# A retention and gMLP kernel on one core: the residual of three of four pairs by DMA transposes, and a new order of all its work

## The chip, the core and the metric

The kernel runs on one core of a Trainium2 chip. The core has engines with instruction lists of their own: PE (TensorE, matrix products into PSUM), DVE (VectorE), ACT (ScalarE), POOL (GpSimd) and SP (SyncE, which here only issues DMA transfers). They wait for one another through semaphores. The metric is the time of one execution on the device in microseconds; less is better.

## The reference

Inputs are q, k and v of 8 sequences, 8 heads, 576 positions and 64 numbers each, and the weights of one gMLP block. The first part is attention without a softmax, with a decay per head; its output, heads side by side, is the block's input x and is also its residual:

```python
scores = scale * np.matmul(q, k.transpose(0, 1, 3, 2))
Dmat = np.where(rel >= 0, gamma[:, None, None] ** rel[None, :, :], 0.0)
x = np.matmul(scores * Dmat, v)              # heads side by side: (8, 576, 512)
h = gelu_tanh(x @ w_in); u, v = h[..., :512], h[..., 512:]
v_n = (v - mean(v)) / sqrt(var(v) + 1e-6) * g_ln
v_s = np.einsum('ts,bsd->btd', w_sg, v_n) + b_sg[None, :, None]
out = x + (u * v_s) @ w_out
```

## The kernel before

Two sequences make a pair, with 1152 rows in 9 tiles of 128 rows; there are 4 pairs (0 to 3) and 36 tiles (0 to 35, nine to a pair). Attention runs over 20 blocks of rows (0 to 19, five to a pair; the middle one is half as long and covers the end of one sequence and the start of the next). The decay is split into factors on q, k and v, and what lies before a block is carried in a running product of k and v.

For each block: SP loads q, k and v (a_load, lines 422 and 425); POOL scales and casts them to bf16 (a_prep, 444 and 450; in block 0 DVE and ACT do a part); PE transposes q and k (a_T, 490), DVE copies that to qkT (499); PE makes the scores (a_S, 522), DVE masks them into ret (535, 538); PE carries the running product (a_Z, 554; ACT copies it to zb, 563) and makes the values (a_O and a_O2, 575); ACT copies the result to xT (a_Oev, 631), the block's input with its channels on the partitions, one xT for a pair, two buffers in all.

For each tile or two: PE multiplies xT by the second half of w_in (m_V, 642), ACT applies the GELU to vg (649), DVE takes mean and variance (657, 658), POOL turns them into factors (662 to 665), ACT normalizes to vn (677). PE multiplies the first half of w_in by xT (m_U, 689), ACT writes the GELU to uT (699). For each sequence PE then multiplies vn by w_sg transposed (m_W, 708; wT is made at the start from wnat, 803 and 807), and DVE gates uT with the result (m_Wg, 718). For each tile m_O makes the output in one PSUM bank: four matmuls of xT with an identity put the residual there (729; they turn xT back to rows), four of uT with w_out add the rest (734). ACT copies the bank to ob (m_Oev, 739), and SP stores it (m_store, 742).

All of this is cut into jobs, one per call of such a function, numbered in the order of `add`. A table, ORDER, lists the job numbers; each engine's instructions stand in the order in which its jobs come in the table, interleaved by `Planner.follow`. The planner's durations only decide how the engines' lists are interleaved while the program is written down; with ORDER given they don't reorder an engine's list. Entries with an f are matmuls on a scratch tile (`warm`, line 332) that keep PE going while it waits for the first loads. PSUM has three banks for the MLP (tag d), two double banks for attention (pp) and one for the running product (zp); loads have 12 buffers, ob has 3.

Of the kernel before, what the change touches and what calls it, by code (L numbers as in the profile page):

```python
# [11 lines left out]
F32 = mybir.dt.float32  # L12
BF = mybir.dt.bfloat16
# [7 lines left out]
SWITCH = {("F", "Q"): 93.0, ("Q", "F"): 125.0}  # L21
# [44 lines left out]
class Job:  # L66
    def __init__(self, eng, dur, due, fn, deps=(), new=None, uses=(), mode=None, nbytes=0, run=0, what="", behind=None, since=0.0, lag=0.0, ins=0, port=False):
        self.what, self.behind, self.since, self.lag, self.ins, self.port = what, behind, since, lag, ins, port
        self.eng, self.dur, self.due, self.fn = eng, dur, due, fn
        self.deps = [d for d in deps if d is not None]  # L70
        self.new = [] if new is None else list(new) if isinstance(new, (list, tuple)) else [new]
        self.mode, self.nbytes, self.run = mode, nbytes, run
        self.start = self.out = None
        for b in uses:
            b.users.append(self)
        for b in self.new:
            b.users.append(self)


class Planner:  # L80
# [50 lines left out]
    def place(self, j, t):  # L131
        j.start = t
        if j.nbytes:
            per = (9.5 + 0.0385 * j.run) * j.nbytes / j.run / 16.0
            room = 160.0 - j.nbytes / j.run / 16.0
            full = 0.0
            for end, n in reversed(self.ring):
                room -= n
                if room < 0:
                    full = end  # L140
                    break
            self.free[j.eng] = max(t + j.dur, full)
            self.dma_free = max(self.dma_free, t + 1500.0) + per
            self.ring.append((self.dma_free, j.nbytes / j.run / 16.0))
            j.out = self.dma_free + 1500.0
            self.dmas.append(j.out)
# [82 lines left out]
def kernel(  # L229
# [31 lines left out]
    BUFS = dict(ld=12, wst=2, qkb=2, vb=3, qkT=2, ret=4, zb=4, xT=2, uT=2, vg=3, mv=3, vn=10, ob=3,  # L261
# [14 lines left out]
    NBK = len(RB)  # L276

# [10 lines left out]
    warm = consts.tile([128, 512], BF, name="warm")  # L288
# [745 lines left out]
```

## Time and profile before

| | us |
|---|---|
| median of 3 runs | 223.44 (221.72 to 223.61) |
| the profiled execution, its own time | 223.99 |
| its span, first to last instruction | 222.3 |
| PE busy | 206.7 (93% of the span) |
| DVE, ACT, POOL busy | 129.7, 138.7, 113.3 |
| moved by DMA | 42.76 MB |

The profile is one execution. A busy PE is counted from matmuls that overlap, so that lengths on PE are read from the chain of waits, which gives each piece only the time until the next; a single row of the timeline is longer than that. A row of the timeline has start, length, engine, line, operation, tiles and count, and in brackets the idle time ahead of it with what ended it. A row of a group has its busy time and the mean in ns behind the first bar, idle time behind the second. The first record of a group of matmuls is sometimes missing.

### The profile page before, as it was taken

The numbers are of one execution on the slowest core, as the hardware profiler recorded it, in microseconds if no ns is written. First come the engines' busy times: TensorE is split into PE (matmuls) and PEld (weight loads), VectorE is DVE, ScalarE is ACT, GpSimd is POOL, SyncE is SP. The second block draws the span as 40 slices with busy tenths as digits, with TensorE's granted clock in tenths as the row PEclk, the third lists the DMA queues.
The fourth block names the chain that finished last, engine by engine and source line by source line (L and its number), as shares of the span: only waits on it lengthen the run. The fifth ranks groups of instructions, "written<-read, shape, count | busy, mean of one in ns | idle before, by whom it ended". The sixth has DMA issues, their size and how long they took to land.

```text
span 222.3 us, 8281 instructions
## 1 busy us (share of the span) xinstructions
PE 206.7 (93%) x3599; PEld 140.9 (63%) x3637; DVE 129.7 (58%) x239; ACT 138.7 (62%) x241; POOL 113.3 (51%) x157
## 2 busy tenths in 40 slices
PE   7689699899999999999999999998999999999992
PEld 2354557677666766677666856676666777567661
DVE  6858246968547806777666464498656476044420
ACT  2577787646775484894664757845657763766232
POOL 5253619788875594759367239744275820022000
PEclk9999999999999999999999999999999999999999
DMA  6999799999999999999898021599010111211333
GB/s 170 269 340 285 214 301 278 297 301 240 302 263 333 251 273 234 253 306 271 208 288 232 6 80 66 182 285 272 26 74 26 49 50 50 95 49 50 142 142 143
DMA packets 70054, 42.76 MB, mean 192 GB/s; under 512 B 14138, under 2 KB 63298, under 8 KB 70018
## 3 DMA queue, kind: packets, MB, share of 16 engines
q1 hardware_dynamic: 70000, 42.23, 68.8%
q8 instruction: 28, 0.46, 0.9%
q14 instruction: 8, 0.07, 0.1%
q10 hardware_dynamic: 18, 0.00, 0.0%
HBM read 32.79 MB, written 9.44 MB: 190 GB/s over the span
## 4 chain that ended last, share of the span: by engine, by line
PE 76%; SPq 8%; DMA 5%; issue 3%; DVE 2%; ACT 2%; POOL 1%; ACTq 0%
PE wp L708 17%; PE op L734 13%; PE hu L689 13%; PE hv L642 12%; PE pp L575 6%; SPq L425 5%; PE op L729 4%; PE pp L522 4%; PE pp L490 4%; DMA wst<-in_moe_w_sg_dram 3%; PE zp L554 3%; DMA ld<-in_q_dram 2%; SPq L355 2%; SPq L422 2%; DVE ret L535 1%
## 5 line engine op out<-in xcount | busy, mean ns | idle before, releaser
L535 DVE TENSOR_TENSOR ret<-pp,msk 128x1024 bf16<-128x1024 f32 x32 | 38.0, 1215 | 11.9 <-PE pp L522 11.9
L450 POOL TENSOR_TENSOR vb<-ld,gqv 128x1024 bf16<-128x1024 f32 (+1 forms) x20 | 34.5, 1730 | 18.0 <-DMA ld<-in_v_dram 11.3
L718 DVE TENSOR_TENSOR uT<-wp,uT 128x288 bf16<-128x288 f32 x64 | 28.0, 450 | 25.4 <-PE wp L708 23.9
L708 PE MATMUL wp<-wT,vn 128*128 128x288 bf16 x256 | 40.9, 286 | 0.1
L450 POOL TENSOR_TENSOR qkb<-ld,gqv 128x1024 bf16<-128x1024 f32 (+1 forms) x19 | 32.7, 1721 | 12.5 <-PE wtp L803 4.9
L689 PE MATMUL hu<-xT,w_in 128*128 128x256 bf16 (+1 forms) x320 | 36.8, 262 | 2.1 <-ACT xT L631 1.3
L642 PE MATMUL hv<-w_in,xT 128*128 128x512 bf16 x128 | 35.2, 380 | 1.0 <-issue 0.2
L499 DVE COPY qkT<-pp 128x2048 bf16<-128x2048 bf16 (+1 forms) x20 | 22.2, 1112 | 23.0 <-PE pp L490 22.7
L631 ACT ACTIVATE xT<-pp 128x512 bf16<-128x512 f32 (+1 forms) x40 | 24.8, 673 | 15.8 <-PE pp L575 13.9
L734 PE MATMUL op<-w_out,uT 128*128 128x512 bf16 x128 | 33.8, 379 | 0.8
L689 PEld LDWEIGHTS <-w_in 128*128 128x128 bf16 x320 | 28.2, 98 | 9.8 <-issue 2.6
L657 DVE BATCH_NORM_STATS2 bst<-vg 128x6 f32<-128x512 f32 x36 | 24.7, 686 | 16.2 <-ACT vg L649 16.2
L739 ACT ACTIVATE ob<-op 128x512 f32<-128x512 f32 x36 | 21.4, 598 | 17.5 <-PE op L734 17.2
L662 POOL TENSOR_SCALAR mv<-mv 128x2 f32<-128x2 f32 (+1 forms) x20 | 4.5, 225 | 53.3 <-DVE mv L658 52.4
L708 PEld LDWEIGHTS <-vn 128*128 128x128 bf16 x256 | 24.6, 98 | 9.0 <-issue 0.3
L649 ACT ACTIVATE vg<-hv 128x512 f32<-128x512 f32 x36 | 21.4, 595 | 11.9 <-PE hv L642 9.0
L677 ACT ACTIVATE vn<-vg,mv 128x512 bf16<-128x512 f32 x32 | 25.0, 809 | 5.0 <-POOL mv L665 4.5
L699 ACT ACTIVATE uT<-hu 128x512 bf16<-128x512 f32 x36 | 21.1, 594 | 10.5 <-PE hu L689 10.1
L642 PEld LDWEIGHTS <-xT 128*128 128x128 bf16 x144 | 13.3, 98 | 11.8 <-ACT xT L631 0.3
L444 POOL CAST qkb<-ld 128x1024 bf16<-128x1024 f32 (+1 forms) x19 | 17.9, 946 | 1.1 <-DMA ld<-in_k_dram 1.1
L708 PE MATMUL wp<-wT,vmid 128*128 128x288 bf16 x64 | 18.4, 287 | 0.0
L734 PEld LDWEIGHTS <-uT 128*128 128x128 bf16 x144 | 12.6, 98 | 8.5 <-DVE uT L718 0.2
(78 smaller groups left out, 245.2 us busy)
## 6 DMA issues: line engine op xcount, KB each, us to landing
out_dram<-ob SPq DMA_DIRECT2D x36, 256.0 KB, 2.1
ld<-in_q_dram SPq DMA_DIRECT2D x16, 512.0 KB, 7.4
ld<-in_k_dram SPq DMA_DIRECT2D x16, 512.0 KB, 6.7
ld<-in_v_dram SPq DMA_DIRECT2D x16, 512.0 KB, 6.5
wst<-in_moe_w_in_dram SPq DMA_DIRECT2D x2, 1024.0 KB
wst<-in_moe_w_sg_dram SPq DMA_DIRECT2D x2, 576.0 KB
ld<-in_q_dram SPq DMA_DIRECT2D x8, 128.0 KB, 7.2
ld<-in_v_dram SPq DMA_DIRECT2D x8, 128.0 KB, 6.4
```

The source lines that it names most:

```text
L450: eng.tensor_tensor(dst, src, g.unsqueeze(3).to_broadcast(list(src.shape)), op=Alu.mult)
L499: ins = nc.vector.tensor_copy(st[b, "qkT"][:].rearrange("p c a k t -> p c (a k t)")[:, :, :w], st.pop((b, "tp"))[:].rearrange("p c a k s t ...
L535: ins = nc.vector.tensor_tensor(ret[:].rearrange("p r (k t) -> p (r k) t", k=2), sc[:].rearrange("p r (k t) -> p (r k) t", k=2), msk2[:].r ...
L631: nc.scalar.activation(dst, src, Act.Copy)
L642: ins = nc.tensor.matmul(hv[:], xTs[p][:, kk, 128 * m:128 * m + 128], w_in[:, kk, F2:], start=(kk == 0), stop=(kk == KK - 1))
L649: unfence(nc.scalar.activation(vgs[i][:], cur.pop(("hv", i))[:], Act.Gelu_apprx_tanh), ("V", i))
L657: nc.vector.bn_stats(bst[:], vgs[i][:])
L677: nc.scalar.activation(vn[:], vg[:], Act.Identity, scale=mv[:, s, 2:3], bias=mv[:, s, 3:4])
L689: ins = nc.tensor.matmul(hu[:, n, :], w_in[:, kk, 128 * c:128 * c + 128], xTs[p][:, kk, 128 * m:128 * m + 128 * w], start=(kk == 0), stop= ...
L708: ins = nc.tensor.matmul(ps[:], vns[t0 + j][e][:, 128 * c:128 * c + 128], wT[e][j][:, half * HS:(half + 1) * HS], start=(j == 0), stop=(j ...
L718: ins = nc.vector.tensor_tensor(uTs[p][:, c, col:col + HS], cur.pop(("wp", b, c, half))[:], uTs[p][:, c, col:col + HS], op=Alu.mult)
L734: ins = nc.tensor.matmul(op[:], uTs[p][:, c, r], w_out[:, c, :], start=False, stop=(c == KK - 1), skip_group_check=True)
```

## The change

The residual of pairs 1 to 3 (27 tiles, XP = 1) no longer goes through PE. A new job m_X on SP issues a DMA transpose of a tile's xT (128 channels by 4 x 128 bf16) into a row tile xr, three buffers; PE does only the four w_out matmuls, and DVE instead of ACT evicts the bank by adding xr to it. Pair 0 keeps the identity matmuls and ACT's copy. xT is laid out tile by tile, so that a tile is one run of 1 KB in each partition. The warm-up tile becomes F32, and one F32 matmul stands for four of before. The planner's durations are new numbers, and the table ORDER is another one throughout, so that every engine's list is reordered.

```diff
-    '0 1 17 2 81 6 82 80 111 f9 83 7 84 112 f6 87 85 3 88 22 114 8 86 90 115 113 9 89 f6 118 116 119 120 f2 12 283 '
+    '0 f9 1 6 81 2 111 83 7 f11 84 112 3 8 85 114 86 120 89 12 f5 115 f5 113 13 116 118 117 f4 121 119 283 123 284 87 '
...
-    BUFS = dict(ld=12, wst=2, qkb=2, vb=3, qkT=2, ret=4, zb=4, xT=2, uT=2, vg=3, mv=3, vn=10, ob=3,
+    BUFS = dict(ld=12, wst=2, qkb=2, vb=3, qkT=2, ret=4, zb=4, xT=2, uT=2, vg=3, mv=3, vn=10, ob=3, xr=3,
...
+    XP = 1
-    warm = consts.tile([128, 512], BF, name="warm")
+    warm = consts.tile([128, 512], F32, name="warm")
...
-            for _ in range(n):
-                nc.tensor.matmul(scr[:], warm[:, :128], warm[:], start=True, stop=True, skip_group_check=True)
+            for w in [512] * (n // 4) + [128 * (n % 4)] * (n % 4 > 0):
+                nc.tensor.matmul(scr[:, :w], warm[:, :128], warm[:, :w], start=True, stop=True, skip_group_check=True)
...
-            xTs[p] = new("xT", [128, KK, NT * 128], BF)
+            xTs[p] = new("xT", [128, NT, KK, 128], BF)
...
-        for j in range(KK):
-            ins = nc.tensor.matmul(op[:, 128 * j:128 * j + 128], xTs[p][:, j, r], ident[:],
-                                   start=(j == 0), stop=False, skip_group_check=True)
+        if p < XP:
+            for j in range(KK):
+                ins = nc.tensor.matmul(op[:, 128 * j:128 * j + 128], xTs[p][:, m, j, :], ident[:],
+                                       start=(j == 0), stop=False, skip_group_check=True)
...
+        for c in range(KK):
+            ins = nc.tensor.matmul(op[:], uTs[p][:, c, r], w_out[:, c, :], start=(p >= XP and c == 0), stop=(c == KK - 1),
+                                   skip_group_check=True)
...
+    def m_X(i):
+        p, m = divmod(i, NT)
+        cur["xr", i] = new("xr", [128, KK, 128], BF)
+        nc.sync.dma_start_transpose(cur["xr", i][:], xTs[p][:, m].rearrange("p j r -> p (j r)"))
+
     def m_Oev(i):
-        unfence(nc.scalar.activation(cur["ob", i][:], cur.pop(("op", i))[:], Act.Copy), ("out", i))
+        op, ob = cur.pop(("op", i)), cur["ob", i]
+        if i // NT < XP:
+            ins = nc.scalar.activation(ob[:], op[:], Act.Copy)
+        else:
+            ins = nc.vector.tensor_tensor(ob[:], op[:], cur.pop(("xr", i))[:].rearrange("p j r -> p (j r)"), op=Alu.add)
+        unfence(ins, ("out", i))
```

Three places of the new order. First DVE at the start. Before, it zeroes vmid, wT and wnat and then scales block 0's q (L450) and begins the column numbers (L752):

```order
L786 MEMSET vmid10_93 64x256
L787 MEMSET vmid11_94 64x256
L781 MEMSET wT0_4_99 64x288
L782 MEMSET wT1_0_100 64x288
L776 MEMSET wnat_74 128x5x32
L777 MEMSET wnat_74 128x5x32
L778 MEMSET wnat_74 64x352
L450 TENSOR_TENSOR qkb_168<-ld_139,gqv_89 128x2x8x64
L752 COPY col_76<-tp_170 128x9
```

The same place on DVE in the changed kernel, where L456 scales q and L771 begins the column numbers:

```order
L805 MEMSET vmid10_93 64x256
L806 MEMSET vmid11_94 64x256
L456 TENSOR_TENSOR qkb_155<-ld_139,gqv_89 128x2x8x64
L771 COPY col_76<-tp_157 128x9
L773 TENSOR_SCALAR colt_78<-col_76 128x4
```

The five memsets of wT and wnat went behind block 1's masks and later.

Second SP at the end of the kernel. Before, only the last stores (tiles 27, 32, 31, 34, 35 and 33) stand there, one behind the other:

```order
L742 DMA out_0_dram<-ob_5060 128x512
L742 DMA out_0_dram<-ob_5071 128x512
L742 DMA out_0_dram<-ob_5083 128x512
L742 DMA out_0_dram<-ob_5118 128x512
L742 DMA out_0_dram<-ob_5128 128x512
L742 DMA out_0_dram<-ob_5140 128x512
```

SP at the end in the changed kernel, from the transpose of tile 31 (xr_4968) on; the transposes of 34, 35 and 33 are xr_5006, xr_5031 and xr_5040, and the stores are those of tiles 29, 32, 31, 34, 35 and 33:

```order
L750 DMA_TRANSPOSE xr_4968<-xT_3889 128x4x128
L761 DMA out_0_dram<-ob_4985 128x512
L750 DMA_TRANSPOSE xr_5006<-xT_3889 128x4x128
L761 DMA out_0_dram<-ob_4992 128x512
L761 DMA out_0_dram<-ob_5000 128x512
L750 DMA_TRANSPOSE xr_5031<-xT_3889 128x4x128
L750 DMA_TRANSPOSE xr_5040<-xT_3889 128x4x128
L761 DMA out_0_dram<-ob_5044 128x512
L761 DMA out_0_dram<-ob_5050 128x512
L761 DMA out_0_dram<-ob_5058 128x512
```

The transposes stand between stores that wait for additions; those of tiles 35 and 33 are behind the store of tile 31.

Third SP around the last transpose of pair 1, tile 13, which is xr_3776 (xT_1540 is pair 1's xT, xT_2768 pair 2's; the three stores ahead of it are those of tiles 14, 12 and 16). The changed kernel has there:

```order
L750 DMA_TRANSPOSE xr_3506<-xT_1540 128x4x128
L428 DMA ld_3599<-in_k_dram 128x8x128
L761 DMA out_0_dram<-ob_3485 128x512
L761 DMA out_0_dram<-ob_3277 128x512
L761 DMA out_0_dram<-ob_3744 128x512
L750 DMA_TRANSPOSE xr_3776<-xT_1540 128x4x128
L428 DMA ld_3786<-in_k_dram 128x8x128
L750 DMA_TRANSPOSE xr_3966<-xT_2768 128x4x128
```

Before, stores and loads alone stand around the stores of pair 1's last tiles:

```order
L742 DMA out_0_dram<-ob_3480 128x512
L742 DMA out_0_dram<-ob_3508 128x512
L742 DMA out_0_dram<-ob_3562 128x512
L422 DMA ld_3620<-in_q_dram 128x8x128
L422 DMA ld_3623<-in_k_dram 128x8x128
L422 DMA ld_3631<-in_k_dram 128x8x128
L742 DMA out_0_dram<-ob_3609 128x512
```

What moved: the reading of xT for the residual, which was on PE inside m_O, is now in SP's queue, behind stores, and ACT's first write of the third xT (xT_3889) waits for the transposes of xT_1540.

More of the change, by code (lines that the diff above doesn't have):

```diff
@@ L66, with __init__ @@
 class Job:
-    def __init__(self, eng, dur, due, fn, deps=(), new=None, uses=(), mode=None, nbytes=0, run=0, what="", behind=None, since=0.0, lag=0.0, ins=0, port=False):
-        self.what, self.behind, self.since, self.lag, self.ins, self.port = what, behind, since, lag, ins, port
+    def __init__(self, eng, dur, due, fn, deps=(), new=None, uses=(), mode=None, nbytes=0, run=0, what="", behind=None, since=0.0, lag=0.0, ins=0, port=False, parts=1):
+        self.what, self.behind, self.since, self.lag, self.ins, self.port, self.parts = what, behind, since, lag, ins, port, parts
         self.eng, self.dur, self.due, self.fn = eng, dur, due, fn
@@ L133, in place @@
         if j.nbytes:
[L134 to L146, printed above, removed]
+            n = j.nbytes / j.run / 16.0 / j.parts
+            at = t
+            for part in range(j.parts):
+                if part and len(self.dmas) >= 8:
+                    at = max(at, self.dmas[-8])
+                room, full = 160.0 - n, 0.0
+                for end, m in reversed(self.ring):
+                    room -= m
+                    if room < 0:
+                        full = end
+                        break
+                self.dma_free = max(self.dma_free, at + 1500.0) + (9.5 + 0.0385 * j.run) * n
+                at = max(at + j.dur / j.parts, full)
+                self.ring.append((self.dma_free, n))
+                j.out = self.dma_free + 1500.0
+                self.dmas.append(j.out)
+            self.free[j.eng] = at
         else:
@@ L641, in m_V @@
         for kk in range(KK):
[L642 removed]
+            ins = nc.tensor.matmul(hv[:], xTs[p][:, m, kk, :], w_in[:, kk, F2:],
                                    start=(kk == 0), stop=(kk == KK - 1))
@@ L819, in loads @@
             J["ld", b, t] = add("SP", 550.0 * (3 - ns), T0[b] - 30000.0, lambda b=b, t=t: a_load(b, t),
-                                new=B_ld[b, t], nbytes=ns * 262144, run=256 * ns)
+                                new=B_ld[b, t], nbytes=ns * 262144, run=256 * ns, parts=3 - ns)
     loads(0)
@@ L834 @@
         j.due = -1e6 + n
-    j_z0 = add("DVE", 1000.0, -6e5, zero_wnat, what="zero")
-    j_z1 = add("DVE", 1200.0, -6e5, zero_vmid, what="zero")
-    j_z2 = add("DVE", 400.0, -5e5, zero_wT)
+    j_z0 = add("DVE", 850.0, -6e5, zero_wnat, what="zero")
+    j_z1 = add("DVE", 1360.0, -6e5, zero_vmid, what="zero")
+    j_z2 = add("DVE", 690.0, -5e5, zero_wT)
     bf = Buf("d")
     j_tc = add("PE", 300.0, 7000.0, to_col, new=bf, since=6000.0, mode="F", ins=2)
-    j_cm = add("DVE", 900.0, 7500.0, col_math, deps=[j_tc], uses=[bf])
+    j_cm = add("DVE", 1650.0, 7500.0, col_math, deps=[j_tc], uses=[bf])
     j_rows = []
@@ L844 @@
         jb = add("PE", 300.0, 15000.0, lambda a=a: to_rows(a), deps=[j_cm], new=bf, mode="F", ins=10)
-        j_rows.append(add("DVE", 650.0, 15500.0, lambda a=a: rows(a), deps=[jb], uses=[bf]))
+        j_rows.append(add("DVE", 430.0, 15500.0, lambda a=a: rows(a), deps=[jb], uses=[bf]))
     j_pv = add("ACT", 2400.0, 16000.0, place_vmid, deps=j_rows[:1] + [j_z1])
@@ L911 @@
         otb = Buf("pp")
-        own = (10 if ns == 2 else 6) * 56.0 * (1 if ns == 2 else .55)
+        own = 600.0 if ns == 2 else 215.0
         st[b, "zs"] = tuple(zs)
@@ L998 @@
                     db, obb = Buf("d"), Buf("ob")
-                    jOut = add("PE", 1090.0, due, lambda i=i: m_O(i), deps=need + wo, new=[db, obb],
-                               uses=[B_x, B_u], mode="F", ins=17)
-                    jOe = add("ACT", 597.0, due + 700.0, lambda i=i: m_Oev(i), deps=[jOut], uses=[db, obb])
+                    if p < XP:
+                        jOut = add("PE", 1090.0, due, lambda i=i: m_O(i), deps=need + wo, new=[db, obb],
+                                   uses=[B_x, B_u], mode="F", ins=17)
+                        jOe = add("ACT", 597.0, due + 700.0, lambda i=i: m_Oev(i), deps=[jOut], uses=[db, obb])
+                    else:
+                        xr = Buf("xr")
+                        jX = add("SP", 1000.0, due - 6000.0, lambda i=i: m_X(i), deps=J["xd", i], new=xr, uses=[B_x],
+                                 nbytes=131072, run=256)
+                        jOut = add("PE", 862.0, due, lambda i=i: m_O(i), deps=need + wo, new=[db, obb],
+                                   uses=[B_u], mode="F", ins=9)
+                        jOe = add("DVE", 640.0, due + 700.0, lambda i=i: m_Oev(i), deps=[jOut, jX], uses=[db, obb, xr])
                     add("SP", 500.0, due + 1000.0, lambda i=i: m_store(i), deps=[jOe], uses=[obb], nbytes=262144, run=2048)
```

35 lines of the change are left out of this document (17 added, 18 removed), and 63 rows, old and new, of the table ORDER.

## The prediction

> **What bounds the kernel now.** I read the page's engine summary first, then the chain that ended last, then busy time by stage, then the chain's last pieces one by one. The summary and the chain's shares by engine:
>
> ```profile
> span 222.3 us, 8281 instructions
> PE 206.7 (93%) x3599; PEld 140.9 (63%) x3637; DVE 129.7 (58%) x239; ACT 138.7 (62%) x241; POOL 113.3 (51%) x157
> PE 76%; SPq 8%; DMA 5%; issue 3%; DVE 2%; ACT 2%; POOL 1%; ACTq 0%
> ```
>
> PE is the limit: 76% of the chain is its own work, and what isn't (SPq and DMA, 13%) is the start, where the weights come in. The stages say when (columns: stretch, its length, busy time of PE, PEld, DVE, ACT, POOL, granted clock, DMA share, GB/s):
>
> ```profile
> 0.00:10.00 10.00, 6.79 (x55) 2.79 (x57) 7.20 (x35) 3.31 (x5) 3.27 (x20) 1.00 0.87 212
> 10.00:20.00 10.00, 8.78 (x205) 5.08 (x200) 7.33 (x8) 8.49 (x13) 5.20 (x4) 1.00 1.10 340
> 20.00:30.00 10.00, 7.92 (x140) 5.05 (x141) 3.38 (x7) 7.16 (x14) 5.08 (x8) 1.00 0.95 236
> 30.00:40.00 10.00, 9.19 (x169) 6.85 (x169) 7.01 (x17) 6.74 (x14) 6.45 (x9) 1.00 0.97 283
> 40.00:200.00 160.00, 155.79 (x2912) 109.04 (x2940) 98.76 (x162) 104.48 (x185) 91.90 (x115) 1.00 0.68 184
> 120.00:140.00 20.00, 19.72 (x360) 13.68 (x361) 11.74 (x21) 13.71 (x25) 10.61 (x18) 1.00 0.24 78
> 140.00:160.00 20.00, 19.02 (x358) 13.40 (x363) 13.72 (x24) 12.07 (x21) 8.82 (x13) 1.00 0.79 212
> 160.00:180.00 20.00, 19.84 (x346) 14.11 (x349) 11.88 (x21) 13.87 (x25) 13.83 (x20) 1.00 0.15 55
> 180.00:200.00 20.00, 19.22 (x303) 12.95 (x305) 8.76 (x16) 12.19 (x22) 1.37 (x4) 1.00 0.14 54
> ```
>
> The clock is full. From 40 to 200 us PE idles only 160 - 155.8 = 4.2 us, so there a saving must be work taken off PE; in the first 40 us it idles 7.3 us while the DMA engines are full. After 120 us they are mostly free, except from 140 to 160.
>
> **The residual.** Pieces of the chain near the end (start, length):
>
> ```profile
> 199.43 0.86 PE hv L642 x4
> 202.22 0.87 PE hu L689 x8
> 205.88 0.61 PE wp L708 x5
> 207.58 2.45 PE wp L708 x20
> 216.21 0.22 PE op L729 x4
> 216.43 0.86 PE op L734 x4
> 218.47 0.60 ACT ob L739
> ```
>
> One output tile costs PE 0.22 us for the four identity matmuls of L729 and 0.86 us for the four of L734. They are in series on the bounding engine, so 27 tiles without L729 save 27 x 0.22 = 5.94 us. Nothing hides this saving; only what replaces the matmuls can eat it.
>
> The eviction moves for the same 27 tiles:
>
> ```profile
> L739 ACT ACTIVATE ob<-op 128x512 f32<-128x512 f32 x36 | 21.4, 598 | 17.5 <-PE op L734 17.2
> L538 DVE TENSOR_TENSOR ret<-pp,msk 128x512 bf16<-128x512 f32 x4 | 2.8, 691 | 2.3 <-PE pp L522 2.3
> L718 DVE TENSOR_TENSOR uT<-wp,uT 128x288 bf16<-128x288 f32 x64 | 28.0, 450 | 25.4 <-PE wp L708 23.9
> ```
>
> An addition of 128x512 from PSUM with a bf16 operand is what L538 does: 691 ns. DVE gains 27 x 0.691 = 18.7 us and ACT loses 27 x 0.598 = 16.1. From 120 to 200 us DVE is busy 46.1 of 80 us; with some 15 of the 18.7 it reaches about three quarters, still under PE. What queues behind an addition there is a gate (L718), a copy of qkT or a mask, each of which feeds PE. At the very end the addition is on the path: +0.09 us. The last gate before tile 34 had 0.22 us of cover from L729; without it the fourth matmul of the tile comes 0.65 us after the last W matmul, against 0.45 us of gate and the hops between engines: at most 0.1 us late, counted at nothing.
>
> **The transposes.** No row shows one. The nearest rows of the same queue, issue to landing:
>
> ```profile
> out_dram<-ob SPq DMA_DIRECT2D x36, 256.0 KB, 2.1
> ld<-in_q_dram SPq DMA_DIRECT2D x16, 512.0 KB, 7.4
> ```
>
> So L, the time of one transpose, lies between 2.1 us (a store, mostly in the free stretch) and 7.4 us (a load in a full queue). It is late only where L exceeds the time that the order leaves. That I count in PE work, from the release of what the transpose waits for to its use. The transposes of the last pair stand in SP's queue behind stores, and a store waits for its own addition. The tightest is tile 35: from the end of tile 31 PE has four W groups (2.45), tile 34 and tile 35 (0.86 each), 4.2 us; less the addition of 31 and its hop (0.9), 3.2 us. Tiles 33 and 34 have 4.1, tile 22 has 4.6, tile 11 about 4.9, most others 6 to 30. One more place isn't an addition at all: xT has two buffers, so pair 3's first write of xT by ACT now waits for all nine transposes of pair 1. The last of them (tile 13) stands behind the store of tile 16. From tile 16 on PE has U (0.87), V (0.86), attention values, U, one output and a transposition group, some 4.7 us, before ACT is asked; less the addition and the store's issue, and with the two outputs that PE still has behind it, L may be about 4. Behind that ACT write wait the norms and GELUs of pair 3 and with them V of tile 28.
>
> I take L near the store's 2.1, since most of them run after 120 us beside a DMA share of 0.14 to 0.24, and allow +1.0 us for those that meet the loads of the 0.79 stretch and for additions that hold up DVE's queue. Ends: 0, and at L = 7.4 in every place (7.4 - 3.2) + (7.4 - 4.0) + (7.4 - 4.6) + (7.4 - 4.9) = 12.9 us.
>
> One rule speaks against the change. The Trainium skill, "VectorE: DVE Perf Modes", in its section on the three transpose paths gives 390 ns for a 128x128 block on TensorE and 1309 ns on the DMA crossbar, and its rules prefer TensorE where PSUM will do as destination, as it does here. In this kernel the TensorE block costs 0.22/4 = 0.055 us in the stream, and no run so far shows the other figure. An estimate from it, four blocks one after another, is L = 5.2 us, and the sum would then hold +4.1 in place of +1.0, about 220.
>
> **The new order.** Every engine's list is another one; three things can be priced. First, the start. Rows by start and length, of the chain, DVE, ACT and PE:
>
> ```profile
> 0.78 4.26 DMA ld<-in_q_dram
> 4.19 0.27 DVE L787 MEMSET vmid<- 64x256 uint32 x1
> 6.12 1.23 DVE L450 TENSOR_TENSOR qkb<-ld,gqv 128x1024 bf16<-128x1024 f32 x1
> 7.06 1.06 ACT L442 ACTIVATE qkb<-ld 128x1024 bf16<-128x1024 f32 x1 [3.26 <-DMA ld<-in_k_dram]
> 8.75 0.17 DVE L762 TENSOR_TENSOR col<-colr,col 128x10 bf16<-128x10 f32 x1
> 8.97 0.66 PE L769 MATMUL tp<-ident,col 128*4 128x128 bf16 x9 [1.50 <-DVE col L762]
> 9.57 0.64 PE L490 MATMUL pp<-ident,qkb 64*128 64x64 bf16 x32
> 31.19 1.26 ACT L386 ACTIVATE wnat<-wst 128x576 bf16<-128x576 f32 x2 [0.78 <-DMA wst<-in_moe_w_sg_dram]
> 42.15 0.65 PE L708 MATMUL wp<-wT,vn 128*128 128x288 bf16 x4
> ```
>
> q lands at 5.04, but DVE finishes zeroing wT and wnat before it scales q at 6.12; then come the column numbers, PE's transposition of them, and the first attention work at 9.57. The new order puts those memsets behind: q's scaling can start at 5.04, and the first attention work 1.1 us earlier (k's cast, done at 8.1, doesn't hold it). Against it, the loads of block 3 now stand ahead of w_sg: 3 x 0.52 MB at the 283 GB/s of that stretch, so w_sg lands some 5.5 us after 31.2, and with it the first W matmul (42.15). But PE has more to do ahead of that: two more V, one more U and the attention of block 4, five builds fewer, 3.4 us more work in all by the chain's lengths. Net -1.1 us; ends -3 (the earlier blocks also fill the 7.3 us of idle time) and +1.9 (5.5 - 3.4 with nothing to put there, less 0.2).
>
> Second, changes between the two kinds of PE work:
>
> ```profile
> 137.37 1.03 PE L734 MATMUL op<-w_out,uT 128*128 128x512 bf16 x4
> 138.33 0.64 PE L522 MATMUL pp<-qkT 64*64 64x128 bf16 x32
> 138.90 0.40 PE L729 MATMUL op<-ident,xT 128*128 128x128 bf16 x4
> ```
>
> L734 takes 0.86 and the scores start after 0.96: 0.10 us to go from full-array to 64-row work, nothing on the way back. The old order has 47 such entries, the new one 41: -0.6 us. Third, the warm-up tile in F32 and xT laid out by tile change no count on the path: the fills (41 units, now 39) sit in waits that stay, and the xT eviction writes the same elements. If an F32 unit weren't as long as four bf16 ones, the idle time would just be longer or shorter by it; the work behind it waits for loads.
>
> **Sum**, on the profiled execution's 223.99 us: -5.94 residual, -1.1 start, -0.6 changes, +0.09 last addition, +1.0 late transposes = -6.55, so 217.4. The median of the runs, 223.44, lies 0.55 lower: 216.9, and I say 217.0.
>
> **Rivals.**
> Late transposes (slower). If a transpose lands as late as a load does in a full queue, or if its four blocks go one after another, it gates the places named above. The loss grows by 4 us for each us of L above 4.9: 4L - 16.7. It eats the other 7.55 us at L = 6.1. At 7.4 the time is 223.44 - 7.55 + 12.9 = 228.8. For it: SP's queue is one line, with stores that wait ahead of them, and three xr buffers. Against it: after 160 us the DMA share is 0.15, and 24 of 27 have over 4.1 us. Chance 0.14, a quarter of it below the crossing. The Trainium skill's figures (page and section as above) would put L below the crossing, at 5.2.
> The new order gives it back. The old order leaves PE 4.2 us idle in 160; a reshuffle of all five lists with a fuller DVE may double that (+4.2), and the start may take the bad end (+1.9). Then 223.44 - 5.94 - 0.6 + 0.1 + 1.9 + 4.2 = 223.1: no change. For it: scores of blocks 1, 2 and 4 come 1.1, 0.6 and 1.2 us of PE work after their transposition, while the copy between them takes 1.1 (0.7 for block 2). Against it: elsewhere the distances are as before or longer. Chance 0.22.
> That the change doesn't do what it says is out: 27 transposes and 27 additions stand in the program.
>
> **Chances and range.** The forecast case has 0.64 and lies between 211.5 (start -3, no late transpose, half of the 4.2 us idle gone) and 219.5. Measurements of this kernel can tell 1%, 2.2 us: 221.2 and 225.7 are the bounds. Faster: 0.64 + 0.03 of the late transposes + 0.07 of the second rival = 0.74. Same: 0.12 of the second, 0.02 of the first: 0.14. Slower: 0.12. To leave out no more than 2 in 10 the range runs to 225.0 above; below, to 211.5.
>
> **What would show it.** Right: L729 down to 36 matmuls; the additions near 0.69 us; no wait of DVE for a transpose over 1 us; PE idle in the middle 160 us no more than 5 us; first attention work near 8.5. Wrong: DVE's additions or ACT's first xT of pair 3 waiting for xr's DMA; SP busy issuing transposes for several us each; the first W after 45 us with PE idle before it; PE waiting for qkT or ret in the new order's early blocks.

## The result and the profile after

The changed kernel takes 215.49 us (median of four runs, 213.49 to 215.86); before takes 222.98 (four runs, 221.72 to 223.61). The ratio is 0.965, 95% interval 0.958 to 0.973: 7.5 us faster, where 217.0 us had been forecast. The profiled execution of the changed kernel took 215.27 us, so it stands near the median. One kernel below, the doubled transposes with six buffers, had two executions in a slow state, over 1.5% above its fastest; its median and its ratio are those of the other two.

The page's first lines and the chain's shares by engine:

```profile
span 213.6 us, 8084 instructions
...
PE 200.2 (94%) x3481; PEld 136.6 (64%) x3514; DVE 147.2 (69%) x266; ACT 124.0 (58%) x214; POOL 113.5 (53%) x157
...
PE 83%; SPq 5%; DMA 5%; issue 3%; POOL 1%; DVE 1%; DVEq 0%; POOLq 0%
```

PE is 6.5 us less busy (206.7 before) and holds more of the chain, 83% instead of 76%. DVE has 17.5 us more and ACT 14.7 less, about what 27 evictions that change engine come to. Busy time by stage, with the columns as before (stretch, length, PE, PEld, DVE, ACT, POOL, clock, DMA share, GB/s):

```profile
0.00:10.00 10.00, 8.49 (x50) 4.30 (x51) 6.21 (x30) 3.04 (x4) 4.24 (x20) 1.00 0.88 227
10.00:20.00 10.00, 8.23 (x187) 4.97 (x187) 7.73 (x10) 7.40 (x11) 3.81 (x4) 1.00 1.17 296
20.00:30.00 10.00, 7.51 (x132) 4.75 (x133) 4.98 (x11) 5.95 (x11) 7.80 (x9) 0.85 1.09 256
30.00:40.00 10.00, 9.82 (x239) 7.56 (x239) 6.46 (x11) 9.09 (x19) 6.06 (x11) 0.98 1.06 306
40.00:200.00 160.00, 157.55 (x2832) 110.30 (x2859) 114.86 (x195) 98.52 (x172) 91.63 (x116) 1.00 0.85 207
120.00:140.00 20.00, 19.84 (x400) 13.68 (x401) 16.25 (x29) 11.62 (x21) 14.63 (x20) 1.00 1.17 245
```

In the middle 160 us PE now idles 160 - 157.55 = 2.45 us, where it was 4.2. Both figures are too large. In either profile 27 of these gaps are 0.05 us each, ahead of a group of V or output matmuls whose first record is missing (PE has x3481 matmuls here for x3514 weight loads, and x3599 for x3637 before). That is 1.4 us of each figure, so that the idle time went from about 2.8 to about 1.0 us. Two things are new: the granted clock is 0.85 from 20 to 30 us, and the DMA engines are full from 120 to 140 us (1.17 instead of 0.24).

The transposes. First the view of tile xr (issue and addition with their durations in ns, minimum, median and maximum; who waited for xr; the time to landing), then the page's row of the additions:

```profile
L750 SPq DMA_TRANSPOSE xr<-xT x27: 1194/1226/3713, 94.1 to 206.7; - x27
...
  DVE ob L757: 1.5, 1
  ACT xT L637: 1.4, 1
...
DMA to landing us min/median/max: 2.4/4.0/7.4
```

```profile
L757 DVE TENSOR_TENSOR ob<-op,xr 128x512 f32<-128x512 f32 x27 | 18.5, 690 | 8.9 <-PE op L741 7.3
```

Only two instructions in the whole run wait for a transpose: one addition, 1.5 us, and ACT's write of xT, 1.4 us. The time to landing counts from the start of the issue, so that the issue is part of it. The addition that waits is the last but one, that of tile 35. The end of the chain (start, length), then SP and DVE there:

```profile
205.42 1.22 SPq L750
...
206.69 2.81 DMA xr<-xT
```

```profile
203.01 1.22 SPq L750 DMA_TRANSPOSE xr<-xT  x1
204.32 1.00 SPq L761 DMA_DIRECT2D out_dram<-ob  x2
205.42 2.53 SPq L750 DMA_TRANSPOSE xr<-xT  x2
```

```profile
203.57 0.69 DVE L757 TENSOR_TENSOR ob<-op,xr 128x512 f32<-128x512 f32 x1 [0.17 <-PE op L741]
...
209.16 1.29 DVE L757 TENSOR_TENSOR ob<-op,xr 128x512 f32<-128x512 f32 x2 [1.51 <-DMA xr<-xT]
```

The addition of tile 31 ends at 204.26. SP has been held by the transpose of tile 34 until then; it issues two stores, and at 205.42 the transpose of tile 35. That of tile 33 follows at 206.69 and lands 2.81 us after its issue began. PE's last matmuls end at 208.7 (11 of L741, 2.62 us from 206.04). The addition of tile 35 has waited 1.5 us when it starts at 209.16, and the last one behind it starts at 209.8, 1.1 us after PE's end.

### The profile page after: what moved, and what is told of

The parts are those of the page before. It is cut to its first block, busy times and chain, and to the rows that moved or that the text cites. A ratio compares the mean times of both kernels' runs of the same rounds, so it can differ in the third digit from the quotient of the medians.

```text
span 213.6 us, 8084 instructions
## 1 busy us (share of the span) xinstructions
PE 200.2 (94%) x3481; PEld 136.6 (64%) x3514; DVE 147.2 (69%) x266; ACT 124.0 (58%) x214; POOL 113.5 (53%) x157
## 4 chain that ended last, share of the span: by engine, by line
PE 83%; SPq 5%; DMA 5%; issue 3%; POOL 1%; DVE 1%; DVEq 0%; POOLq 0%
PE wp L714 18%; PE hu L695 16%; PE hv L648 14%; PE op L741 13%; PE pp L581 7%; PE pp L496 4%; PE pp L528 4%; DMA ld<-in_q_dram 4%; PE zp L560 4%; SPq L428 3%; PE wtp L822 1%; DMA xr<-xT 1%; PE op L736 1%; SPq L431 1%; SPq L361 1%
## 5 line engine op out<-in xcount | busy, mean ns | idle before, releaser
L456 POOL TENSOR_TENSOR qkb<-ld,gqv 128x1024 bf16<-128x1024 f32 (+1 forms) x19 | 32.7, 1721 | 21.0 <-DMA ld<-in_q_dram 11.1
L695 PE MATMUL hu<-xT,w_in 128*128 128x256 bf16 (+1 forms) x320 | 38.0, 265 | 0.0
L456 POOL TENSOR_TENSOR vb<-ld,gqv 128x1024 bf16<-128x1024 f32 (+1 forms) x20 | 34.6, 1730 | 5.7 <-PE pp L581 3.4
L648 PE MATMUL hv<-w_in,xT 128*128 128x512 bf16 x125 | 35.9, 387 | 1.8 <-issue 0.7
L741 PE MATMUL op<-w_out,uT 128*128 128x512 bf16 x130 | 34.3, 380 | 0.7
L757 DVE TENSOR_TENSOR ob<-op,xr 128x512 f32<-128x512 f32 x27 | 18.5, 690 | 8.9 <-PE op L741 7.3
L648 PEld LDWEIGHTS <-xT 128*128 128x128 bf16 x144 | 13.9, 100 | 12.7 <-issue 1.1
L741 PEld LDWEIGHTS <-uT 128*128 128x128 bf16 x144 | 13.0, 98 | 12.3 <-DVE uT L724 0.4
L569 ACT ACTIVATE zb<-zp 128x256 bf16<-128x256 f32 x32 | 12.2, 383 | 14.0 <-PE zp L560 13.9
```

Source lines behind the costliest of these rows:

```text
L456: eng.tensor_tensor(dst, src, g.unsqueeze(3).to_broadcast(list(src.shape)), op=Alu.mult)
L648: ins = nc.tensor.matmul(hv[:], xTs[p][:, m, kk, :], w_in[:, kk, F2:], start=(kk == 0), stop=(kk == KK - 1))
L695: ins = nc.tensor.matmul(hu[:, n, :], w_in[:, kk, 128 * c:128 * c + 128], xTs[p][:, m:m + w, kk, :], start=(kk == 0), stop=(kk == KK - 1), ...
L741: ins = nc.tensor.matmul(op[:], uTs[p][:, c, r], w_out[:, c, :], start=(p >= XP and c == 0), stop=(c == KK - 1), skip_group_check=True)
```

## The experiments

Each was timed beside the kernel before on one chip; that kernel's median lay between 222.75 and 222.97 us in these comparisons.

### The new order without the transposes' residual

The residual of all four pairs goes through PE and ACT again, with the changed kernel's order, and its transposes left out of it.

```diff
-    XP = 1
+    XP = 4
```

> The new order with the old residual: identity matmuls on PE and ACT's copy for all four pairs, no transposes (ACT's copies stand where DVE's additions stood in the order). Theory: the 7.5 us between the medians (222.98 and 215.49) are 5.9 of residual and the rest order and start, less about 1 us that the end waits for the last transposes. Then this kernel takes about 215.5 + 5.9 - 0.9 = 220.5 us. Rival: the order is what made the kernel fast, and the residual was mostly eaten by the transposes: 218 us or less.

Measured: 219.56 us (218.79 to 220.37), ratio 0.985 (0.980 to 0.991), 0.9 us below the theory. Its middle stage:

```profile
40.00:200.00 160.00, 159.79 (x2906) 111.80 (x2906) 100.53 (x170) 106.68 (x190) 90.67 (x116) 1.00 0.66 185
```

From 40 to 200 us PE idles 0.2 us; no record is missing in this profile (x3622 of both), so this is to be set against the 2.8 above. The order alone is worth 3.3 us, twice the 1.7 of the forecast.

### The residual with the old order

The changed kernel with the order of before, the transposes put into it: each behind the addition of the tile three outputs earlier. Its place in SP's queue is then ahead of that tile's store.

> The old order with the new residual: each transpose stands in SP's queue behind the addition of the third tile before, the additions stand on DVE where ACT's copies stood. Theory: PE loses 5.9 us of work here too, and some 1 to 2 us come back as waits for transposes, for which this order leaves no room of its own: 218 to 219 us. Rival: without an order made for it the transposes and DVE's additions eat all of it: 222 us or more.

Measured: 222.12 us (ten runs, 220.72 to 223.99), ratio 0.997 (0.993 to 1.001), the rival's time. The time that the saving should have given is missed by over 3 us; hardly anything of the 5.9 us can be seen. SP's longest waits (us in sum, times, longest), and one of DVE's:

```profile
SPq L750 <- DVE ob L757: 28.6, 7, 10.3
SPq L750 <- DVE uT L724: 16.2, 7, 8.5
```

```profile
DVE ob L757 <- DMA out_dram<-ob: 3.9, 5, 1.0
```

SP stands at a transpose that waits for its buffer, and the stores and loads behind it stand too; DVE then waits for ob, whose stores have not gone out. The next kernel puts each transpose behind the store of the tile five outputs earlier, and gives xr six buffers:

```diff
-L761 DMA out_dram<-ob 128x512 x2
+L761 DMA out_dram<-ob 128x512
+L750 DMA_TRANSPOSE xr<-xT 128x4x128
+L761 DMA out_dram<-ob 128x512
 L750 DMA_TRANSPOSE xr<-xT 128x4x128
...
+L761 DMA out_dram<-ob 128x512
 L750 DMA_TRANSPOSE xr<-xT 128x4x128
-L761 DMA out_dram<-ob 128x512
```

> The job order of before, with the residual of pairs 1 to 3 through transposes, as in the run residual_alone, but each transpose now stands in SP's queue behind the store of the output tile five tiles earlier (so it no longer holds a store or a load behind it), with 6 xr buffers instead of 3. Theory (the 5.9 us of PE work are saved in either order, and residual_alone lost them again because its transposes stood ahead of stores and loads in SP's queue): 217 to 218.5 us, and no wait of VectorE for ob's stores longer than 1 us in sum. Rival (the old order has no use for a shorter PE stage, since its late stage then waits for loads, softmax work and norms of pair 3 instead, so that only the new order turns the saving into time): 221 us or more, with PE idle in 160 to 200 us for want of work from POOL, ACT or loads while no wait for a transpose or a store stands ahead of them.

Measured: 219.53 us (219.06 to 220.18), ratio 0.986 (0.982 to 0.990). It lies between the two expectations. The place in SP's queue and the three more buffers together were worth 2.6 us, and the waits of DVE for xr and ob are gone, but only 3.3 of the 5.9 us are there. PE waits in the middle now (1.04 us at 122.84, among others), behind POOL's preparation of block inputs, and that waits for a load (POOL, then SP):

```profile
117.05 1.04 POOL L450 CAST qkb<-ld 128x1024 bf16<-128x1024 f32 x1 [2.32 <-DMA ld<-in_k_dram]
```

```profile
101.89 4.51 SPq L750 DMA_TRANSPOSE xr<-xT  x3
...
110.12 0.79 SPq L428 DMA_DIRECT2D ld<-in_k_dram  x1
```

To tell the transposes in the queue from the old order itself, a kernel with that order and no transposes: DVE adds a fixed tile of w_out, the residual of pairs 1 to 3 is left out.

```diff
-            ins = nc.vector.tensor_tensor(ob[:], op[:], cur.pop(("xr", i))[:].rearrange("p j r -> p (j r)"), op=Alu.add)
+            ins = nc.vector.tensor_tensor(ob[:], op[:], w_out[:, 0, :], op=Alu.add)
```

> The job order of before, with no residual matmul and no transpose for pairs 1 to 3: VectorE adds a fixed tile of w_out in place of the attention output, so the residual of pairs 1 to 3 is left out. It is to no_transpose what residual_alone2 is to the changed kernel. Theory (of the 5.9 us of PE work that go, the old order gives back 2.6 us because SP's queue, with 27 transposes in it, issues the loads of pairs 2 and 3 later, so that POOL's preparation at 112 to 122 us holds PE up): without transposes 216.5 to 217.5 us. Rival (the old order gives them back by itself, because POOL, ACT and VectorE set the time of its late stage once PE is shorter): 218.5 to 220 us, with PE idle in 80 to 160 us as in residual_alone2.

Measured: 217.14 us (five runs, 216.60 to 218.20), ratio 0.975 (0.971 to 0.979): the theory. The same cast on POOL starts 2.5 us earlier and waits for nothing; its load of k went out 6.5 us earlier, with no transposes ahead of it:

```profile
114.58 1.04 POOL L449 CAST qkb<-ld 128x1024 bf16<-128x1024 f32 x1
```

```profile
103.66 0.68 SPq L427 DMA_DIRECT2D ld<-in_k_dram  x1
```

So the old order does turn the shorter PE work into time (5.6 us), and 27 transposes in SP's queue take 2.4 of it back. This load is the place where the traces show how; that it is the whole of the 2.4 us is not shown.

### The changed kernel without transposes, and with copies

The same edit of the addition with the new order, the transposes left out of the table; the residual of pairs 1 to 3 is again left out.

> The changed kernel without its 27 transposes: DVE adds a weight tile instead of the residual, so the residual of pairs 1 to 3 is left out. Theory: the transposes cost only the two waits that the trace shows, 1.5 us of DVE at the end (0.9 of the end) and 1.4 of ACT ahead of pair 3: 214 to 214.6 us, and the loads are no faster. Rival: the transposes also slow the loads or hold up SP through the second half: 212.5 us or less.

Measured: 214.37 us (213.43 to 215.67), ratio 0.964 (0.958 to 0.970). That is the theory's time. The transposes in the changed kernel cost 1.1 us by this, within the scatter of both.

A plain copy at each transpose's place moves the same bytes without turning them:

```diff
-        nc.sync.dma_start_transpose(cur["xr", i][:], xTs[p][:, m].rearrange("p j r -> p (j r)"))
+        nc.sync.dma_start(cur["xr", i][:], xTs[p][:, m])
```

> The changed kernel with a plain copy from xT to xr in place of each transpose, of the same bytes and at the same place of SP's queue (the residual of pairs 1 to 3 is then added untransposed, so the output is another one). If it is the transposing that makes the data late (many small packets), a copy lands in 2 to 2.5 us in the median instead of 4.0 and the time comes near the one without transposes, 214.3 to 214.8 us. If it is the place in the queue and the gate, whatever the kind of transfer, the time stays at 215.2 to 215.8 us and the last addition still waits over 1 us.

Measured: 213.30 us (212.02 to 214.73), ratio 0.958 (0.952 to 0.964). The view of tile xr:

```profile
L750 SPq DMA_DIRECT2D xr<-xT x27: 470/471/1626, 93.4 to 205.1; - x27
...
DMA to landing us min/median/max: 2.0/2.7/6.3
```

SP issues a copy in 0.47 us where a transpose takes 1.23, and the data land 2.7 us after the start of the issue instead of 4.0; no addition and no write of xT waits for it. So the waits come from the transposing, its issue included, and not from the place in the queue. The landing is 0.2 us above the range that was expected, and the time 1 us below; the intervals of this ratio and of the changed kernel's overlap.

### Each transpose twice

```diff
-        cur["xr", i] = new("xr", [128, KK, 128], BF)
-        nc.sync.dma_start_transpose(cur["xr", i][:], xTs[p][:, m].rearrange("p j r -> p (j r)"))
+        x2 = new("xr", [128, 2, KK, 128], BF)
+        cur["xr", i] = x2[:, 0]
+        for a in range(2):
+            nc.sync.dma_start_transpose(x2[:, a], xTs[p][:, m].rearrange("p j r -> p (j r)"))
```

> The changed kernel with each of the 27 transposes issued twice, the second into the other half of a tile of double size (the addition reads the first half). SP issues 27 more transposes of about 1.2 us, and 3.5 MB more go through the DMA engines. Theory (late transposes are what the change pays, at the two places where the trace shows a wait for xr, the last tile above all): the last transpose is released by the same gate, 1.2 us of issue and 1 to 3 us of transfer come on top of it, and stores stand 1.2 us later behind them: 217 to 219 us. Rival (transposes are hidden nearly everywhere, and the doubled ones fall into SP's idle time and spare DMA share): 215.5 to 216.3 us.

Measured: 229.55 us (228.78 to 230.47), ratio 1.030 (1.025 to 1.035). Both expectations are far off: the first 27 transposes cost 1 to 2.5 us, the next 27 cost 14. DVE waits 7.3 us for xr, but four times only, 5.6 of it behind 195 us, and PE idles from 120 to 160 us as well (35.22 of 40 us busy). Whether lateness in the queue makes this, or the issuing itself, the same doubling in the kernel with six buffers (next section) was to tell; the tile xs that nothing reads has two buffers:

```diff
-        nc.sync.dma_start_transpose(cur["xr", i][:], xTs[p][:, m].rearrange("p j r -> p (j r)"))
+        xs = new("xs", [128, KK, 128], BF)
+        for z in (xs, cur["xr", i]):
+            nc.sync.dma_start_transpose(z[:], xTs[p][:, m].rearrange("p j r -> p (j r)"))
```

> The kernel of the run xr6 (6 xr buffers, 22 of the 27 transposes earlier), with each transpose issued a second time into a tile that nothing reads, ahead of the one that is used. Theory (in the run twice the 14 us came from the pairs of transposes standing late in SP's queue, where stores, loads and the last additions waited behind them; with six buffers most of the pairs have been issued before that): 213.5 to 216 us. Rival (3.5 MB more of small packets and 27 more SP issues of 1.25 us cost what they cost wherever they stand, because loads of pairs 2 and 3 land later): 222 us or more, with PE waiting between 110 and 160 us for work that waits for loads.

Measured: 229.46 us (228.66 and 230.26; the other two executions took 232.44 and 233.66), ratio 1.027 (1.017 to 1.037). My theory fell and the rival's time came: early transposes don't help when there are 54. SP around 125 us, here and in the kernel with six buffers:

```profile
125.46 2.24 SPq L752 DMA_TRANSPOSE xs<-xT  x1
127.80 1.21 SPq L752 DMA_TRANSPOSE xr<-xT  x1
129.06 0.58 SPq L428 DMA_DIRECT2D ld<-in_k_dram  x1
129.70 1.04 SPq L763 DMA_DIRECT2D out_dram<-ob  x2
```

```profile
113.36 6.63 SPq L750 DMA_TRANSPOSE xr<-xT  x4
120.08 0.53 SPq L428 DMA_DIRECT2D ld<-in_k_dram  x1
120.67 1.04 SPq L761 DMA_DIRECT2D out_dram<-ob  x2
```

Four pairs of transposes, from 114.50 on, hold the load of k and two stores back by 9 us. What follows is on DVE and then on PE:

```profile
134.42 0.69 DVE L759 TENSOR_TENSOR ob<-op,xr 128x512 f32<-128x512 f32 x1 [7.42 <-DMA out_dram<-ob]
```

```profile
135.16 0.40 PE L714 MATMUL wp<-wT,vmid 128*128 128x288 bf16 x1 [6.01 <-DVE ob L759]
```

An addition waits 7.4 us for an ob buffer whose store has not gone out. The next W group needs the PSUM bank that this addition empties (the MLP has three), and PE stops for 6 us until it ends. From 110 to 160 us PE is busy for 42.01 of 50 us (the kernel with six buffers: 50.00), at a granted clock of 0.93. So 6 of the 8 us that PE idles there are this one wait for a store; the rival had named the loads alone. POOL's casts wait for loads of k too, up to 11 us. Another reading would be that 3.5 MB more make every transfer slower. The traces don't show that: from issue to landing the large loads of q, k and v take 6.7, 7.0 and 6.1 us in the median here, and 7.0, 8.1 and 6.6 with six buffers and single transposes. They are issued later. By these traces the price is paid in SP's queue: the issue of a transpose delays every load and store behind it, and that costs nothing until their slack is used up.

### Six buffers

The changed kernel with three more xr buffers; 22 of the 27 transposes move forward in the order, each behind the addition that frees its buffer, so that none stands among the last six stores:

```diff
-    BUFS = dict(ld=12, wst=2, qkb=2, vb=3, qkT=2, ret=4, zb=4, xT=2, uT=2, vg=3, mv=3, vn=10, ob=3, xr=3,
+    BUFS = dict(ld=12, wst=2, qkb=2, vb=3, qkT=2, ret=4, zb=4, xT=2, uT=2, vg=3, mv=3, vn=10, ob=3, xr=6,
```

> The changed kernel with six buffers for the transposed tiles instead of three, and 22 of the 27 transposes moved forward in SP's queue (behind the fifth addition before, and behind the eviction that writes their tile). Theory: the waits at the end and ahead of pair 3 go, 214 to 214.6 us, as without transposes. Rival: earlier transposes meet the loads of pairs 2 and 3 in the queue and POOL waits for those: 215.5 us or more.

Measured: 212.84 us (212.22 to 214.02), ratio 0.956 (0.951 to 0.961), over a microsecond better than expected. Run again beside the one with a longer fill:

> The kernel of the run xr6 unchanged, beside xr6_fill on the same chip, so that the two can be compared and the best version has eight executions: 212.3 to 213.4 us.

Measured: 213.20 us (212.23 to 213.59), ratio 0.955 (0.948 to 0.961). The eight executions lie between 212.2 and 214.0 us, with a median of 213.1: 2.4 us under the changed kernel, and the best version found. The view of tile xr and the end of its chain:

```profile
L750 SPq DMA_TRANSPOSE xr<-xT x27: 1191/1264/3667, 93.9 to 199.7; - x27
...
DMA to landing us min/median/max: 2.4/4.0/8.5
```

```profile
205.87 2.68 PE op L741 x12
...
208.58 0.69 DVE ob L757
```

The transposes land no earlier after their issue, up to 8.5 us, but none is waited for, and the last addition starts as PE ends. In this profile PE's last matmuls end at 208.55, in the changed kernel's at 208.7, and the last addition starts at 208.58 instead of 209.8. Between these two executions nearly all of the difference is the wait at the end, 1.1 of 1.2 us.

### The fills and the clock

The changed kernel without its last fill, and the kernel with six buffers with that fill longer. The first:

```diff
-    ... 293 122 f5 126 295 ...
+    ... 293 122 126 295 ...
```

> The changed kernel without its last fill unit (1.24 us of dummy matmuls at 20.8 us, between the second half of the first hv work and the next attention part). Theory (TensorE's granted clock falls after a stretch in which PE has little work, as at 26 to 32 us in the changed kernel's profile): PE is idle about 1.2 us more between 20 and 23 us, the clock of the 26 to 32 us slices falls in most executions, the run's mean clock is 0.985 or less, and the time is 215.5 to 218 us. Rival (the drop has nothing to do with idle time on PE): clocks of 0.987 to 0.995 as in the runs of the changed kernel, time 215.0 to 215.8 us.

Measured: 214.63 us (214.03 to 215.70), ratio 0.964 (0.960 to 0.969), at mean clocks of 0.971 to 0.981 in its four executions; the changed kernel's four had 0.987 to 0.995. The clock fell, as expected; the time did not rise. The second:

```diff
-    ... 293 122 f5 126 295 ...
+    ... 293 122 f8 126 295 ...
```

> The kernel of the run xr6 with the last fill unit, at about 20.5 us, of 8 units instead of 5 (about 0.65 us more of dummy matmuls, so that PE's idle time before 22.8 us is some 0.5 us instead of 1.1). Theory (the granted clock falls after a stretch of some microseconds in which PE idles for more than about 1 us): the clock stays at 0.99 to 1.00 in every execution; as the work of 20 to 34 us waits for loads and casts anyway (fill_out lost nothing in time at clocks of 0.971 to 0.981), the time is that of xr6 within 0.6 us, 212.2 to 213.4 us. Rival (the clock drop does cost time when it falls on the first hv and hu work): 211.2 to 212.2 us, faster than xr6.

Measured: 213.46 us (212.46 to 213.87), ratio 0.955 (0.949 to 0.961), as without the longer fill; the clock was 0.990 to 0.992 in all four, so the drop did not go away. What these two show of the clock is told at the end.

## Why the prediction was right

The forecast was 217.0 us and the kernel takes 215.49. The runs make a small table of medians in us:

| | order of before | new order |
|---|---|---|
| residual on PE | 222.9 | 219.56 |
| no residual matmuls, no transposes | 217.14 | 214.37 |
| with transposes, three buffers | 222.12 | 215.49 |
| with transposes, six buffers | 219.53 | 213.1 |

**The residual** (-5.94, with +0.09 for the last addition: -5.85). Down the columns, from the first line to the second, it is worth 5.8 and 5.2 us. The term holds; L736, the identity matmuls that are left, stands at 36, and the additions take 690 ns.

**The new order** (-1.1 for the start and -0.6 for the changes between kinds of work: -1.7). Across the first two lines it is worth 3.3 and 2.8 us. This is the term that was mis-sized. What failed is the sum's silence on the idle time in the middle, which stood only in the range: the step read it as 4.2 us, 1.4 of which are missing records; of the other 2.8 the new order alone leaves 0.2, and the changed kernel about 1.0. No run times the -0.6 by itself. Across the last two lines the order is worth 6.6 and 6.4 us, so that the two parts of the change don't simply add: the old order has little room for transposes in SP's queue, and where they stand there was not planned with it. The lower end of the range was added up wrongly: its terms give 211.9 us, not 211.5. The order's start came out otherwise than the step had it. DVE scales q as forecast, but the first attention work follows only at 9.09 us (forecast near 8.5). DVE's row, then PE's:

```profile
5.03 1.23 DVE L456 TENSOR_TENSOR qkb<-ld,gqv 128x1024 bf16<-128x1024 f32 x1 [0.57 <-DMA ld<-in_q_dram]
```

```profile
6.75 2.10 PE L338 MATMUL scr<-warm 128*128 128x512 f32 x5
8.77 0.39 PE L788 MATMUL tp<-ident,col 128*4 128x128 bf16 x4
9.09 0.64 PE L496 MATMUL pp<-ident,qkb 64*128 64x64 bf16 x32
45.20 0.66 PE L714 MATMUL wp<-wT,vn 128*128 128x288 bf16 x4
```

The fills on PE last until 8.8 us, while DVE is done with the column numbers at 7.85 (0.18 from 7.67): that the fills "sit in waits that stay" was wrong by most of a microsecond here. The first W group stands at 45.20 instead of 42.15, 3.05 us later where the step counted 3.4 us of work more ahead of it; with six buffers it stands at 43.99, and with the new order alone at 44.27, so that the start is worth 0.35 us in this execution and 1.3 to 1.6 in those, around the 1.1.

**The late transposes** (+1.0, ends 0 and 12.9). By the kernel without transposes it is 1.1 us, and by the ends of two profiles (six buffers, above) 1.1 as well. By the plain copy and by six buffers, which both lie below the kernel without any, it would be 2.2 to 2.4. Why they are faster than a kernel that has less to do I can't say; their intervals overlap with its own. The two places where something waits are those that the step named, the last addition and ACT's xT in pair 3, which was also on the list of what would speak against the forecast: it waits, but 1.4 us. DVE's wait of 1.5 us is over the 1 us that the list allowed. What was wrong is how the size came out right, and that it did is in part luck. L was taken near 2.1 us because the DMA engines would be free. They weren't: their share from 120 to 140 us is 1.17, where it is 0.49 in the new order without transposes and 0.79 with copies, so that the transposes themselves fill them. The median of L is 4.0. The +1.0 was allowed for other things, loads and additions in DVE's queue. And the issue of what stands ahead in SP's queue was not in the sum at all. For tile 35 it is 1.2 us, from the end of tile 31's addition at 204.26 to 205.42, with up to 3.7 us of transpose behind it. These 4.9 us are 1.7 more than the slack of 3.2; its addition waited 1.5. Most of the others have so much slack that a larger L costs nothing. The estimate of 5.2 from the Trainium skill ("VectorE: DVE Perf Modes", three transpose paths), four blocks of 1309 ns, lies above the median of 4.0 and within the 2.4 to 7.4 that the view shows; its sum, 220 us, did not come.

**The rival of late transposes** did not come with 27 of them, but its mechanism is real, and its place is another: not the four tight tiles, as the formula 4L - 16.7 had it, but SP's issue ahead of stores and loads. What stands behind a transpose in SP's queue is weighed nowhere in the prediction; the runs with doubled transposes lose 14 to 16 us, in the traces at such places above all, and the old order loses 2.4 us with single ones.

**The rival that the order gives it back** had idle time going up from 4.2 to 8.4 us. It went down, and the fuller DVE (16.25 of 20 us from 120 to 140) held up no matmul that the trace shows: a weight load for scores waited 0.4 us for an addition, once. At the last gate before tile 34, counted at nothing with at most 0.1 us, PE's weight loads waited 0.4 us as well, and its matmuls went on without a gap.

## What to carry to other kernels

Work taken off the bounding engine becomes time only as far as its replacement finds room in the queue that issues it: count the issue time of each DMA (1.2 us for a transpose here, 0.47 for a copy) and ask which loads and stores stand behind it. Buffers that let a transfer be issued early take its wait away (2.4 us between the medians here, 1.1 of it seen at the end of the traces), but not its issue time: doubled, the same transposes cost 14 to 16 us, early or late. Where a change comes with a new order, time the order by itself.

## What the hardware showed besides

**The clock.** In the changed kernel's profile the granted clock falls to half at 26 to 32 us (stages as above); in the kernel without the last fill it is low from 22 to 28 us, after a wait of PE. The stages of the first, then of the second with that wait:

```profile
26.00:28.00 2.00, 1.39 (x14) 1.07 (x14) 0.43 (x1) 0.96 (x2) 1.01 (x1) 0.76 0.90 168
28.00:30.00 2.00, 1.78 (x6) 0.81 (x6) 0.00 (x0) 0.87 (x2) 1.87 (x2) 0.50 1.13 212
```

```profile
22.00:24.00 2.00, 1.24 (x40) 1.08 (x43) 0.16 (x2) 0.57 (x2) 1.83 (x4) 0.51 1.13 332
```

```profile
22.76 0.63 PE L560 MATMUL zp<-vb,qkb 64*64 64x64 bf16 x16 [2.78 <-POOL vb L456]
```

The Trainium skill ("TensorE: Matmul & The Clock Gate", "Why this matters for your kernels") asks for no idle gap of PE above about 3 us. Here the clock fell with no gap above 1.53 us in the changed kernel and 2.78 in the other. But a gap by itself doesn't decide it: with six buffers and the longer fill it fell to 0.50 after gaps of at most 0.97 us, and in the second profile with six buffers and the fill as it was it stayed full after one of 1.37. What decides it stays open. This early in the kernel it costs no time that a run shows: without the last fill the clock was lower than in the changed kernel and the time no longer. Where PE's work is the path it does cost. In the kernel with six buffers and doubled transposes the clock is 0.50 from 219 to 222 us, shortly after PE has waited 2.5 us for an addition, and the last twelve output matmuls take 4.44 us where the twelve before them took 2.75 (PE, start and length):

```profile
209.97 2.75 PE L741 MATMUL op<-w_out,uT 128*128 128x512 bf16 x12
...
218.59 4.44 PE L741 MATMUL op<-w_out,uT 128*128 128x512 bf16 x12
```

So a part of what the doubled transposes cost there, some 1.7 us, is the slower clock.

**Fetching instructions.** PE's two longest gaps between 10 and 40 us have no releaser in the trace:

```profile
19.59 0.41 PE L528 MATMUL pp<-qkT 64*64 64x128 bf16 x15 [1.35 <-issue]
...
26.61 0.28 PE L560 MATMUL zp<-vb,qkb 64*64 64x64 bf16 x7 [1.53 <-issue]
```

```profile
q8 instruction: 27, 0.44, 1.0%
```

27 packets of 0.44 MB are 16 KB each. PE has 3514 weight loads and as many matmuls, and the two gaps stand 128 pairs, 256 instructions, apart. In the trace's packets of this queue one ends at 18.20 us and the next at 25.18, and both times PE goes on 1.4 us later. The Trainium skill ("Runtime: NRT & Kernel Launch", "Instruction fetch mechanics") has an engine's instructions fetched in blocks of 16 KiB, 256 of them, mostly hidden. The size agrees. That these gaps are such fetches, late because the DMA engines are full (share 1.1 to 1.2 there), fits all of this but no run changes it; if so, they are not hidden here.
